# Stores of a planned kernel ordered two microseconds later, and a crossbar turn planned to land later

## The chip, the cores and the metric

One core of a Trainium2 chip runs the whole program. The metric is the device time of one execution in microseconds (us); lower is better. The engines that matter here are TensorE (PE for its matmuls, PEld for its weight loads), VectorE (DVE), ScalarE (ACT) and SyncE (SP), whose queue issues every DMA of this kernel. GpSimd (POOL) does small things.

## The reference

Eight sequences of 576 tokens go through attention in chunks of 64, a feed-forward net with a residual, and a gated convolution:

```python
scores = scale * np.matmul(q_c, k_c.transpose(0, 1, 2, 4, 3))
attn = softmax(scores); out = np.matmul(attn, v_c)          # 8 heads of 64, chunks of 64
...
xn = (x - mu) / np.sqrt(var + 1e-06) * g_ln
x = x + np.maximum(xn @ w_ch1, 0.0) @ w_ch2                 # 512 -> 2048 -> 512
...
gate_pre += conv_w[k][None, None, :] * xp[:, k:k + S, :]    # 5 taps along the tokens
gate = 1.0 / (1.0 + np.exp(-gate_pre))
return (gate * (x @ w_val)) @ w_out
```

## The kernel before

The 4608 tokens are cut into 9 blocks of 512 (b = 0 to 8) and 36 attention units of 128 tokens. Numbers are split into a high and a low part, so that a product is three matmuls. Blocks 0 and 1 go through the feed-forward net plainly. From block 2 on its first layer is done by Strassen's scheme: for each group g of 512 hidden columns seven products, named 2, 1, 6, 5, 3, 7, 4 (`hidden`, line 1303), each 12 matmuls of 256 columns. Their combined weights lie in HBM (`a_dram`) and are loaded, 512 KB for each product, into a ring of six rooms (names `late_a`, `load` at line 1325, DMA at L1327). Results go from PSUM through ACT (`shot`, L1347), DVE (`join`, L1354), and ACT and DVE again (`high` L1382, `low` L1385) into the second layer (L1412 to L1414).

When a block's output X is complete, `conv` (line 1616) does two things with it beside the next blocks. It computes the five taps of the gate: one ACT step (L1638) and four DVE steps (L1645) for each of four column groups f, in two rooms `u0` and `u1` by turns, and stores the result to HBM (`gd`, L1658). And `seven` (line 1424) makes the seven operands of the last stage: DVE differences (L1454), ACT high parts (L1472), DVE low parts (L1477), and a store of each (`x7d`, L1482) out of three rooms. A room is free again when its store has landed. Block 0's part is done later, from a copy in HBM (`x2d`): `seven_again` reloads it at L1525 and `conv_again` at L1577. The last stage (`val`, `proj`) reloads operands and gates.

From unit 8 on the attention probabilities are turned by a crossbar DMA: ACT takes the halves of the words apart (L682), SP issues the DMA transpose (L690), ACT puts them together (`pT`, L699).

No order is written by hand. Each step is an `Op` with an engine, a duration, dependencies and a priority, and `Plan.run` (line 55) plays them through as a list scheduler: an engine that is free takes the ready step of least priority value. The order of these picks is the order in which the instructions are emitted, and on the chip each engine keeps it: a step that waits holds up everything behind it on its engine, and SP's queue is one such order. An op becomes ready at the planned end of its dependency plus a hop: 80 ns behind DVE or ACT, 220 ns behind PE, 3500 ns behind an SP op (its landing), plus `more` of the op that ended. `slack` of the waiting op is added where the dependency is an SP op. These numbers alone decide the order; none of them is waited for on the chip, where semaphores do that.

Of the kernel before, what the change touches and what calls it, by code (L numbers as in the profile page):

```python
# [20 lines left out]


class Op:
    __slots__ = ("eng", "dur", "fn", "deps", "pri", "left", "after", "ready", "seq", "xfer", "more", "slack")

    def __init__(self, eng, dur, fn, deps, pri, seq):
        self.eng, self.dur, self.fn, self.pri, self.seq = eng, dur, fn, pri, seq
        self.deps = [d for d in dict.fromkeys(deps) if d is not None]
        self.after, self.ready, self.xfer, self.more, self.slack = [], 0.0, None, 0.0, 0.0


class Plan:
# [23 lines left out]
    def run(self):  # L56
        for op in self.ops:
            op.left = len(op.deps)
            for d in op.deps:
                d.after.append(op)  # L60
        free = {e: 740.0 if e == "SP" else 0.0 for op in self.ops for e in op.eng}
        ready = {e: [] for e in free}
        events = []
        done = set()

        def offer(op):
            for e in op.eng:
                heapq.heappush(ready[e], (op.pri, op.seq, op))

        for op in self.ops:  # L70
            if not op.left:
                offer(op)
        t, n, moved, landed = 0.0, 0, 0.0, []
        while n < len(self.ops):
            for e in free:
                if free[e] > t:
                    continue
                q = ready[e]
                while q and q[0][2].seq in done:
                    heapq.heappop(q)  # L80
                if not q:
                    spent = self.idle(t) if self.idle and e == "PE" else None
                    if spent:
                        free[e] = t + spent
                        heapq.heappush(events, (free[e], -1, None))
                    continue
                op = heapq.heappop(q)[2]
                done.add(op.seq)
                dur = op.dur[op.eng.index(e)] if isinstance(op.dur, tuple) else op.dur
                end = t  # L90
                for x, parts in op.xfer or ():
                    flying = landed[-self.LANES :]
                    if len(flying) == self.LANES:
                        end = max(end, flying[0][0])
                    for l, _ in flying:
                        if sum(m for z, m in flying if z > end) + parts > self.RING:
                            end = max(end, l)
                    turn = self.TURN if parts == P and landed and landed[-1][1] != P else 0.0
                    end += dur
                    moved = max(end + self.LAG, moved + turn) + x  # L100
                    landed.append((moved, parts))
                if not op.xfer:
                    end = t + dur
                free[e] = end
                if len(op.eng) > 1:
                    op.fn(e)
                else:
                    op.fn()
                n += 1
                for a in op.after:  # L110
                    if op.xfer:
                        wait = moved - end
                    else:
                        wait = 0.0 if a.eng == (e,) else max(self.HOP[e], self.HOP["PE"] if "PE" in a.eng else 0.0) + op.more
                        if e == "SP":
                            wait += a.slack
                    a.ready = max(a.ready, end + wait)
                    a.left -= 1
                    if not a.left:
                        heapq.heappush(events, (a.ready, a.seq, a))  # L120
                heapq.heappush(events, (free[e], -1, None))
            if n == len(self.ops):
                break
            t = max(t, events[0][0])
            while events and events[0][0] <= t:
                op = heapq.heappop(events)[2]
                if op is not None:
                    offer(op)
# [3 lines left out]
def chunk_attention_ffn_gated_conv(  # L132
# [385 lines left out]
    def unit(u):  # L518
# [3 lines left out]
        b, o = divmod(u, TB)  # L522
# [412 lines left out]
        def turned_probabilities():  # L935
            sp = op("ACT", 1250, apart, ex, bu)
            cp = op("SP", 600, crossbar, sp, su, p=pri - 20000.0)
            cp.more = 1000.0
            return op("ACT", 1370, together, cp)

        ep = turned_probabilities() if ready else None
# [490 lines left out]
    def seven(b, quad, reads, pri):  # L1432
# [29 lines left out]
        def split(i, m, src, *deps):  # L1462
# [21 lines left out]
            oh = add("ACT", 680, high, list(deps) + take(rt), pri)  # L1484
            ol = add("DVE", 690, low, [oh], pri)
            x7_store[b, m] = add("SP", 1300, store, [ol], pri)
            x7_store[b, m].more = 2000.0
            hold(rt, x7_store[b, m])
            if src:
# [81 lines left out]
    def conv_again(f):  # L1571
# [35 lines left out]
            oa = add("DVE", 760, more(i), [oa], pri)  # L1607
        hold(rt, oa)
        conv_store[0, f] = add("SP", 728, keep, [oa], pri)
        hold(at, conv_store[0, f])  # L1610

    def conv(b):
# [19 lines left out]
        for f in range(KD if b else 0):  # L1632
# [31 lines left out]
                oa = add("DVE", 760, more(i), [oa], pri)  # L1664
            last.append(oa)
            conv_store[b, f] = add("SP", 728, keep, [oa], pri)
            hold(at, conv_store[b, f])
        if b == 0:
            x2_store[b] = add("SP", 2900, store, done, pri)
# [441 lines left out]
```

## Time and profile before

| what | us |
|---|---|
| median of 3 runs | 1070.41 |
| lowest and highest | 1068.20, 1075.63 |
| profiled execution | 1070.03 |
| its span, first to last instruction | 1068.2 |

The rows below come from the profiled execution. Of its 1070.03 us the span is 1068.2; 1.83 us lie around it. The granted TensorE clock is 1.00 of full speed over the span, so no step of time is due to the clock. "Idle before" in a row is the time in which that engine did nothing before the instruction, with the instruction or DMA that ended it. A PE matmul's own duration contains its way through the array, so two that follow each other overlap: 12 matmuls of a product start over about 1.4 us.

### The profile page before, as it was taken

The page shows a single profiled execution, that of the slowest core. Times are in us where ns is not written, and L with a number is a line of the kernel's source. Part 1 is how long each engine was busy: PE and PEld are TensorE (multiplying, and loading weights), DVE is VectorE, ACT ScalarE, POOL GpSimd, SP SyncE. Part 2 cuts the span into 40 slices and gives each one's busy share as a digit, 9 for nine tenths or more (in the row PEclk, how much of TensorE's full clock was granted, in tenths as well). Part 3 has the DMA queues.
Part 4 walks back from the last instruction along what each step waited for, and adds up shares of the span by engine and source line. Part 5 has one row for each costly group of instructions (what it writes and reads, how often), then busy time and mean ns, then how long its engine had stood idle before and what let it go on. Part 6 is the DMA issues. An engine that isn't in the chain of part 4 may idle for free.

```text
span 1068.2 us, 22725 instructions
## 1 busy us (share of the span) xinstructions
PE 1053.9 (99%) x8950; PEld 951.4 (89%) x8950; DVE 856.4 (80%) x1464; ACT 540.3 (51%) x871; POOL 40.4 (4%) x77
## 2 busy tenths in 40 slices
PE   9999999999999999999999999999999999999998
PEld 8988888888899988889888898899898989999998
DVE  5888978888885888767878877878756889998785
ACT  5796634435354445445445543544443555655553
POOL 1011000000000000000000000000000000000000
PEclk9999999999999999999999999999999999999999
DMA  8995358667999899989989989998976988999852
GB/s 193 289 368 175 108 159 252 220 179 207 246 329 270 233 297 337 282 242 344 278 260 329 299 233 233 352 282 250 319 234 203 381 330 305 309 334 377 316 206 80
DMA packets 205905, 284.14 MB, mean 266 GB/s; under 512 B 99278, under 2 KB 151014, under 8 KB 205798
## 3 DMA queue, kind: packets, MB, share of 16 engines
q1 hardware_dynamic: 205798, 282.68, 84.6%
q8 instruction: 71, 1.16, 0.5%
q14 instruction: 36, 0.29, 0.1%
HBM read 207.64 MB, written 67.63 MB: 258 GB/s over the span
## 4 chain that ended last, share of the span: by engine, by line
PE 88%; DMA 4%; issue 2%; DVE 2%; ACT 2%; SPq 1%; POOL 0%; DVEq 0%; ACTq 0%; POOLq 0%
PE m L1255 24%; PE o L1255 8%; PE v L1255 8%; PE y L1034 7%; PE yA L1412 5%; PE yA L1414 5%; PE yB L1412 5%; PE yB L1414 4%; PE yA L1413 4%; PE yB L1413 4%; PE att L631 3%; PE att L604 3%; PE h L1010 3%; PE h L1012 2%; PE h L1011 2%
## 5 line engine op out<-in xcount | busy, mean ns | idle before, releaser
L1255 PEld LDWEIGHTS m<-late,late_a 128*128 128x128 f32 x2352 | 296.3, 188 | 22.5 <-DVE c_hl L1354 6.1
L1255 PE MATMUL m<-late,late_a 128*128 128x256 f32 x2352 | 303.3, 280 | 7.1 <-DMA late_a<-a 3.1
L1645 DVE SCALAR_TENSOR_TENSOR u_room<-X,cw_sb,u_room 128x516 f32<-128x516 f32 (+1 forms) x128 | 95.1, 747 | 10.4 <-ACT u_room L1638 7.9
L1034 PE MATMUL y<-hh,w 128*128 128x512 f32 x224 | 70.9, 398 | 0.0
L1354 DVE TENSOR_TENSOR c_hh<-c_hh,m 128x512 f32<-128x512 f32 x56 | 38.4, 685 | 36.6 <-PE m L1255 22.9
L1347 ACT ACTIVATE c_hh<-m 128x512 f32<-128x512 f32 x56 | 33.4, 596 | 54.9 <-PE m L1255 54.7
L1412 PE MATMUL yA<-late_h,w 128*128 128x512 f32 x148 | 59.4, 401 | 0.0
L1412 PE MATMUL yB<-late_h,w 128*128 128x512 f32 x148 | 59.0, 399 | 0.0
L1414 PE MATMUL yB<-late_h,w 128*128 128x512 f32 x148 | 58.1, 393 | 0.0
L1414 PE MATMUL yA<-late_h,w 128*128 128x512 f32 x148 | 58.0, 392 | 0.0
L1413 PE MATMUL yA<-late_h,w 128*128 128x512 f32 x148 | 58.0, 392 | 0.0
L1413 PE MATMUL yB<-late_h,w 128*128 128x512 f32 x148 | 57.8, 390 | 0.0
L1034 PEld LDWEIGHTS y<-hh,w 128*128 128x128 f32 x224 | 40.8, 188 | 8.4
L1287 ACT ACTIVATE late<-xs 128x512 fp32r<-128x512 f32 x49 | 30.4, 628 | 35.1 <-PE m L1255 20.6
L1010 PE MATMUL h<-xnt,w 128*128 128x512 f32 x112 | 45.4, 405 | 0.0
L770 POOL TENSOR_TENSOR rstd<-ve,neg_half 128x1 f32<-128x1 f32 x36 | 24.7, 687 | 541.8 <-DVE ve L750 541.4
L1012 PE MATMUL h<-xnt,w 128*128 128x512 f32 x112 | 44.2, 395 | 0.0
L1011 PE MATMUL h<-xnt,w 128*128 128x512 f32 x112 | 44.2, 394 | 0.0
L1034 PE MATMUL y<-hl,w 128*128 128x512 f32 x112 | 44.0, 393 | 0.0
L1382 ACT ACTIVATE late_h<-c_hh 128x512 fp32r<-128x512 f32 x38 | 23.9, 630 | 38.9 <-DVE c_hh L1354 38.2
L678 ACT ACTIVATE p<-p 128x512 f32<-128x512 f32 x33 | 20.8, 630 | 41.6 <-DVE p L670 23.6
L699 ACT ACTIVATE pT<-px 128x1024 uint16<-128x1024 uint16 x28 | 38.5, 1374 | 6.3 <-DMA px<-ps 6.1
(272 smaller groups left out, 2440.0 us busy)
## 6 DMA issues: line engine op xcount, KB each, us to landing
late_a<-a SPq DMA_DIRECT2D x196, 512.0 KB, 5.6
x7d<-late_x SPq DMA_DIRECT2D x42, 512.0 KB, 5.9
late_a<-x7d SPq DMA_DIRECT2D x39, 512.0 KB, 5.4
raw<-in_moe_w_ch_dram SPq DMA_DIRECT2D x32, 512.0 KB, 7.6
late<-x7d SPq DMA_DIRECT2D x24, 512.0 KB, 5.5
qk_room<-in_q_dram SPq DMA_DIRECT2D x100, 112.0 KB, 5.2
qk_room<-in_k_dram SPq DMA_DIRECT2D x100, 112.0 KB, 4.1
x7d<-x SPq DMA_DIRECT2D x21, 512.0 KB, 5.6
```

Source lines behind the costliest of these rows:

```text
L699: nc.scalar.activation(out=t.bitcast(U16).rearrange("p (x s) -> p s x", s=2), in_=st["turned"], func=AF.Copy)
L1010: nc.tensor.matmul(ps, wh, xh, start=(kk == 0), stop=False)
L1011: nc.tensor.matmul(ps, wh, xl, start=False, stop=False)
L1012: nc.tensor.matmul(ps, wl, xh, start=False, stop=(kk == KD - 1))
L1034: nc.tensor.matmul(ps, w[:, s], x, start=opens and n == 0, stop=closes and n == 2, skip_group_check=not b)
L1255: nc.tensor.matmul(ps[:, f], l, right(r, k), start=new and f == k == i == 0, stop=k == 1 and i == 2, skip_group_check=True,)
L1347: nc.scalar.activation(out=st[tag], in_=st[into], func=AF.Copy)
L1354: nc.vector.tensor_tensor(out=st[tag], in0=st[tag], in1=y, op=op)
L1412: nc.tensor.matmul(ps, wh, hh, start=opens and f == 0, stop=False)
L1413: nc.tensor.matmul(ps, wl, hh, start=False, stop=False)
L1414: nc.tensor.matmul(ps, wh, hl, start=False, stop=closes and f == 3)
L1645: nc.vector.scalar_tensor_tensor(out=a, in0=X[b][:, f, i : i + L], scalar=cw_sb[:, i, f : f + 1], in1=a, op0=ALU.mult, op1=ALU.add,)
```

## The change

An `Op` gets a field `behind`, zero by default. Where an op waits for a step that was not on SP, its planned ready time is put off by `behind`. It is set to 2000 ns for three kinds of store: the operands (`x7d`, L1482), the gates of block 0 (L1600) and the gates of the other blocks (L1658). The second edit raises `more` of the crossbar DMA from 1000 to 2500 ns, so the step that puts the turned words together is planned to be ready 6.0 us behind the DMA's issue step, where it was 4.5.

```diff
+                        else:
+                            wait += a.behind
...
-            cp.more = 1000.0
+            cp.more = 2500.0
...
             x7_store[b, m] = add("SP", 1300, store, [ol], pri)
+            x7_store[b, m].behind = 2000.0
             x7_store[b, m].more = 2000.0
...
         conv_store[0, f] = add("SP", 728, keep, [oa], pri)
+        conv_store[0, f].behind = 2000.0
...
             conv_store[b, f] = add("SP", 728, keep, [oa], pri)
+            conv_store[b, f].behind = 2000.0
```

Every engine issues the same instructions as before, in the same number; POOL's order is unchanged, and PE, DVE, ACT and SP have rows in other places from about unit 9 on. Nothing is moved ahead of that. Line numbers grow by 2 to 5.

The first place is PE at the turn from block 1's plain net to block 2's products. `h1_15` is the last hidden column tile of block 1, `m1_2_0` and `m2_2_0` are products 1 and 2 of block 2, group 0. Before:

```order
L1255 MATMUL m1_2_0_2957<-late0_1912,late_a2_0_2_2135 128x256 x12
L1010 MATMUL h1_15_2907<-xnt1_0_1206,w27_1619 128x512
L1011 MATMUL h1_15_2907<-xnt1_0_1206,w27_1619 128x512
L1012 MATMUL h1_15_2907<-xnt1_0_1206,w27_1619 128x512
L1255 MATMUL m2_2_0_2989<-late0_1912,late_a2_0_2_2135 128x256 x12
```

After, on PE at the same place:

```order
L1012 MATMUL h1_15_2899<-xnt1_0_1206,w27_1619 128x512
L1013 MATMUL h1_15_2899<-xnt1_0_1206,w27_1619 128x512
L1014 MATMUL h1_15_2899<-xnt1_0_1206,w27_1619 128x512
L1257 MATMUL m1_2_0_2963<-late0_1912,late_a2_0_2_2148 128x256 x12
L1257 MATMUL m2_2_0_2979<-late0_1912,late_a2_0_2_2148 128x256 x12
```

Product 1 now stands between the last matmuls of `h1_15` and product 2; before it stood ahead of both.

The second place is SP in block 6, group 2, while block 5's gates and operands are stored. `a3_1` is the weight of product 1 of group 3, `gd5` and `x7d5` are the stores of block 5. Before:

```order
L1482 DMA x7d5_2_120<-late_x7_1_1_3132 128x1024
L1327 DMA late_a2_0_2_2135<-a3_2_207 128x1024
L1658 DMA gd5_80<-u_room_185 128x320
L1658 DMA gd5_80<-u_room_185 128x192
L1327 DMA late_a2_0_6_2162<-a3_1_208 128x1024
L1482 DMA x7d5_6_122<-x7_5_6_7962 128x1024
L1327 DMA late_a2_0_6_2162<-a3_6_209 128x1024
L1482 DMA x7d5_3_124<-late_x7_1_1_3132 128x1024
```

After, on SP at the same place:

```order
L1484 DMA x7d5_2_120<-late_x7_1_1_3134 128x1024
L1329 DMA late_a2_0_2_2148<-a3_2_207 128x1024
L1329 DMA late_a2_0_6_2175<-a3_1_208 128x1024
L1329 DMA late_a2_0_6_2175<-a3_6_209 128x1024
L565 DMA qk_room_148<-in_q_dram 32x4x224 x4
L1662 DMA gd5_80<-u_room_185 128x320
L1662 DMA gd5_80<-u_room_185 128x192
L1484 DMA x7d5_6_122<-x7_5_6_7987 128x1024
L1484 DMA x7d5_3_124<-late_x7_1_1_3134 128x1024
```

Two weight loads and four reads of q now go ahead of the gate store that they stood behind.

The third place is block 5, group 1, from product 7 to product 4 on PE, and what DVE does there. `att27` is an attention unit's small products, `m1_5_1` with `late1` is product 7, with `late2` product 4, and `m1_5_2` is product 1 of the next group. PE before:

```order
L1255 MATMUL m1_5_1_6410<-late1_2982,late_a2_0_2_2135 128x256 x12
L631 MATMUL att27_6672<-v26_6500,pT26_6609 64x64 x16
L631 MATMUL att27_6672<-kT27_6607,qT27_6564 64x64 x16
L1255 MATMUL m1_5_2_6707<-late0_1912,late_a2_0_6_2162 128x256 x12
L1255 MATMUL m1_5_1_6410<-late2_3004,late_a2_0_2_2135 128x256 x12
```

PE after:

```order
L1257 MATMUL m1_5_1_6390<-late1_2959,late_a2_0_2_2148 128x256 x12
L633 MATMUL att27_6672<-v26_6503,pT26_6637 64x64 x16
L633 MATMUL att27_6672<-kT27_6605,qT27_6579 64x64 x16
L1414 MATMUL yA_5_6429<-late_h2_1_0_3289,w12_1072 128x512
L1415 MATMUL yA_5_6429<-late_h2_1_0_3289,w12_1072 128x512
L1416 MATMUL yA_5_6429<-late_h2_1_0_3289,w12_1072 128x512
L1257 MATMUL m1_5_1_6390<-late2_3043,late_a2_0_2_2148 128x256 x12
```

Three matmuls of the second layer take the place of the next group's product 1 between 7 and 4. On DVE the sum that product 4 waits for is `c5_1_hl0`, and product 1 of the next group waits for `c5_1_hh1`. DVE before:

```order
L1477 TENSOR_TENSOR late_x7_1_1_3132<-X4_4717,late_x7_1_1_3132 128x512
L1645 SCALAR_TENSOR_TENSOR u_room_185<-X4_4717,cw_sb_74,u_room_185 128x516 x2
L1354 TENSOR_TENSOR c5_1_hh1_6587<-c5_1_hh1_6587,m5_5_1_6594 128x512
L1645 SCALAR_TENSOR_TENSOR u_room_185<-X4_4717,cw_sb_74,u_room_185 128x516 x2
L1354 TENSOR_TENSOR c5_1_hl0_6623<-c5_1_hl0_6623,m1_5_1_6410 128x512
```

DVE after:

```order
L1356 TENSOR_TENSOR c5_1_hh1_6586<-c5_1_hh1_6586,m5_5_1_6592 128x512
L1479 TENSOR_TENSOR x7_4_5_6645<-t4_6623,x7_4_5_6645 128x512
L1649 SCALAR_TENSOR_TENSOR u_room_185<-X4_4717,cw_sb_74,u_room_185 128x516
L1387 SCALAR_TENSOR_TENSOR late_h2_1_0_3289<-c5_1_hh1_6586,late_h2_1_0_3289 128x2x256
L1356 TENSOR_TENSOR c5_1_hl0_6617<-c5_1_hl0_6617,m1_5_1_6390 128x512
```

Four tap steps stood ahead of `c5_1_hl0` and two ahead of `c5_1_hh1`; now one stands ahead of the first and none ahead of the second. Block 6, group 1 has the same move on PE; on DVE there the two taps ahead of `c6_1_hl0` become one tap and one low part (L1385).

## Rows read from the trace of the kernel before

**Rows 1.** The page's first part: busy time, share of the span and instructions of each engine.

```profile
PE 1053.9 (99%) x8950; PEld 951.4 (89%) x8950; DVE 856.4 (80%) x1464; ACT 540.3 (51%) x871; POOL 40.4 (4%) x77
```

**Rows 2.** Windows: us; PE, PEld, DVE, ACT, POOL busy (instructions); clock; DMA share; GB/s.

```profile
100.00:250.00 150.00, 148.59 (x1140) 120.93 (x1139) 124.38 (x225) 69.42 (x106) 8.00 (x17) 1.00 0.59 176
250.00:850.00 600.00, 594.22 (x5080) 534.11 (x5078) 474.37 (x825) 284.63 (x459) 21.76 (x36) 1.00 0.93 281
850.00:1064.00 214.00, 213.77 (x1738) 208.53 (x1736) 176.35 (x282) 115.22 (x204) 0.00 (x0) 1.00 0.80 287
```

**Rows 3.** Waits of PE: who waited for whom, us in total, times, longest.

```profile
PE m L1255 <- DMA late_a<-a: 3.1, 2, 1.6
PE m L1255 <- DVE c_hl L1354: 2.1, 3, 1.0
```

**Rows 4.** Timeline at the turn to block 2: start, us, what [idle before, releaser].

```profile
244.13 1.58 PE L1255 MATMUL m<-late,late_a 128*128 128x256 f32 x12
...
245.54 0.39 PE L1010 MATMUL h<-xnt,w 128*128 128x512 f32 x1
...
246.01 0.39 PE L1012 MATMUL h<-xnt,w 128*128 128x512 f32 x1
...
247.07 0.69 DVE L1022 SCALAR_TENSOR_TENSOR hl<-h,hh 128x512 fp32r<-128x512 f32 x1 [3.22 <-ACT hh L1018]
...
247.81 0.86 PE L1255 MATMUL m<-late,late_a 128*128 128x256 f32 x5 [1.41 <-DVE hl L1022]
```

**Rows 5.** Timeline of SP, block 6, group 2, and of PE there.

```profile
667.95 0.59 SPq L1327 DMA_DIRECT2D late_a<-a  x1
670.99 0.86 SPq L1658 DMA_DIRECT2D gd<-u_room  x2
671.95 0.44 SPq L1327 DMA_DIRECT2D late_a<-a  x1
...
678.15 2.12 PE L1255 MATMUL m<-late,late_a 128*128 128x256 f32 x16 [1.46 <-DMA late_a<-a]
```

**Rows 6.** The window around rows 5, columns as in rows 2.

```profile
665.00:680.00 15.00, 13.54 (x91) 12.27 (x91) 11.16 (x19) 7.32 (x13) 1.49 (x2) 1.00 1.07 362
```

**Rows 7.** Timeline of block 5, group 1.

```profile
558.48 0.73 ACT L1638 ACTIVATE u_room<-X,cw_sb 128x516 f32<-128x516 f32 x1 [2.39 <-DMA gd<-u_room]
...
559.25 1.55 DVE L1645 SCALAR_TENSOR_TENSOR u_room<-X,cw_sb,u_room 128x516 f32<-128x516 f32 x2 [2.42 <-ACT u_room L1638]
...
561.45 1.68 PE L1255 MATMUL m<-late,late_a 128*128 128x256 f32 x12 [0.49 <-DVE c_hh L1354]
...
563.51 1.68 PE L1255 MATMUL m<-late,late_a 128*128 128x256 f32 x12 [0.38 <-DVE c_hl L1354]
```

**Rows 8.** Timeline of block 6, group 1.

```profile
653.31 0.72 ACT L1638 ACTIVATE u_room<-X,cw_sb 128x516 f32<-128x516 f32 x1 [4.88 <-DMA gd<-u_room]
...
655.53 0.68 DVE L1354 TENSOR_TENSOR c_hl<-c_hl,m 128x512 f32<-128x512 f32 x1
...
656.27 1.65 PE L1255 MATMUL m<-late,late_a 128*128 128x256 f32 x12 [0.78 <-DVE c_hl L1354]
```

**Rows 9.** Timeline of SP, block 3, group 2, and of PE there.

```profile
389.31 0.38 SPq L1525 DMA_DIRECT2D u_room<-x2d  x1
...
390.77 0.42 SPq L1327 DMA_DIRECT2D late_a<-a  x1
...
396.87 0.36 PE L1255 MATMUL m<-late,late_a 128*128 128x256 f32 x1 [1.61 <-DMA late_a<-a]
```

**Rows 10.** Waits of ACT: as rows 3.

```profile
ACT u_room L1638 <- DMA gd<-u_room: 25.8, 10, 5.8
...
ACT pT L699 <- DMA px<-ps: 6.1, 5, 2.4
```

**Rows 11.** Timeline of SP and PE, block 4, group 0.

```profile
425.13 1.00 SPq L1525 DMA_DIRECT2D u_room<-x2d  x1
...
429.49 1.55 PE L1255 MATMUL m<-late,late_a 128*128 128x256 f32 x12
```

More of the change, by code (lines that the diff above doesn't have):

```diff
@@ L23 @@
 class Op:
-    __slots__ = ("eng", "dur", "fn", "deps", "pri", "left", "after", "ready", "seq", "xfer", "more", "slack")
+    __slots__ = ("eng", "dur", "fn", "deps", "pri", "left", "after", "ready", "seq", "xfer", "more", "slack", "behind")
     def __init__(self, eng, dur, fn, deps, pri, seq):
@@ L28, in __init__ @@
         self.deps = [d for d in dict.fromkeys(deps) if d is not None]
-        self.after, self.ready, self.xfer, self.more, self.slack = [], 0.0, None, 0.0, 0.0
+        self.after, self.ready, self.xfer, self.more, self.slack, self.behind = [], 0.0, None, 0.0, 0.0, 0.0
 class Plan:
```

## The prediction

> **What bounds the kernel now.** I read the page's busy line first. TensorE's matmuls are busy for 1053.9 us, 99% of the span of 1068.2, no other engine for more than 80% beside its weight loads [rows 1]. So the reader should see at once how little a new order can win: PE's instructions are the same in number and kind, and only its idle time, 1068.2 - 1053.9 = 14.3 us, is to be had. The windows say where that lies. The order changes from about unit 9 on, so the stretch from 100 us to the last matmul counts: there PE is idle for 1.41 + 5.78 + 0.23 = 7.42 us [rows 2]. The other 6.9 us lie in the first 100 us, where no instruction moves, and behind the last matmul. A measurement of this kernel can tell about 1% from no change, which is 10.7 us; even with every idle microsecond in reach gone, the change stays inside that on the fast side.
>
> The waits of PE come next. The largest are two waits for a product's weights (3.1 us in two), then sums that DVE makes for a product (2.1 us in three) [rows 3]; then comes one wait for a low part at the turn to block 2 (1.41) [rows 4]. I looked each of them up in the timeline, because a store planned later can help a wait only where that store, or the order that follows from it, stands in that wait's chain.
>
> **The change part by part.** It removes and adds nothing; each part is a move.
>
> The turn to block 2. Product 2 needs the bank out of which DVE's low part of h1_15 reads. The last matmul of h1_15 starts at 246.01, the low part ends at 247.07 + 0.69 = 247.76, and product 2 starts at 247.81 after 1.41 us of idleness [rows 4]. In the new order product 1 stands between. Its 12 matmuls took from 244.13 to 245.54, 1.41 us [rows 4], and fill just the time that was idle. Term: -1.4; bounds -1.41, the whole wait, and 0, should the low part be later by as much because product 1's own operand or weight is not there.
>
> The weight load in block 6. The load that releases product 1 of group 3 was issued at 671.95, behind a gate store that SP held from 667.95 + 0.59 on and issued at 670.99, when DVE had ended its last tap; PE started the product at 678.15, 6.2 us behind the issue, after 1.46 us of idleness [rows 5]. Now the load stands straight behind the one of 667.95, ahead of that store. The six-room ring allows it: the room's last reader is product 6 of group 2, which PE has left by then. So it goes out at about 668.6, 3.3 us sooner, and a landing 3.3 us sooner covers 1.46. Term: -1.46; bounds -1.46 and 0. The zero is real: in this window the DMA engines show a share of 1.07 and 362 GB/s [rows 6], so a load that starts sooner may wait in the engines instead of in SP's queue. Against that stands that the bytes of the gate store and of an operand's store are now behind it, and I take the full term, being twice covered. The Trainium skill (DMA: Bandwidth & Descriptors, Where 436 GB/s comes from) puts the limit between HBM and SBUF at about 358 GB/s for one core, which this window's 362 has reached; by that rule alone the order of issues in such a window gains nothing and the term would be 0.
>
> What the four q reads and the two gate store pieces now wait for is off PE's path: q is turned more than a group later, and the gates are read back in the last stage.
>
> Block 5, group 1. ACT's tap step waited 2.39 us for a gate store's landing, and DVE's taps behind it; PE then stood 0.49 us for c_hh and 0.38 us for c_hl [rows 7]. In the new order c_hh is ahead of the taps, so its 0.49 goes. Product 4 comes sooner in PE's order: PE is free of the attention unit at 561.45 - 0.49 = 560.96, and three second-layer matmuls of 512 columns, which start 0.23 us apart (245.54 to 246.01 for two [rows 4]), put it at 561.65. The gate store that ACT waits for now stands behind one more load, some 0.5 us of issue; ACT's step would then end at 558.9 + 0.7 = 559.6, one tap of 1.55 / 2 = 0.77 at 560.4, a low part and the sum (0.68 each, as the sum in rows 8) at 561.7. So about 0.1 us of idleness is left of 0.87. Term: -0.75; bounds -0.87 and +0.5.
>
> Block 6, group 1. Here the move costs. ACT's wait for the gate store is 4.88 us, DVE's sum c_hl, behind the taps, runs at 655.53 and PE waits 0.78 us for it [rows 8]. That store keeps its place in SP's queue, so the landing stays. A low part takes the second tap's place ahead of c_hl, 0.1 us less. But three matmuls (0.69 us) stand between products 7 and 4 where a product of 1.4 us stood, so PE arrives 0.7 us sooner at the same wait. Term: +0.6; bounds 0 and +0.7.
>
> Block 3, group 2. PE waits 1.61 us for a weight issued at 390.77, just behind a reload of x2d at 389.31 which itself waits until the gate store of the room that it fills has landed [rows 9]. In the new order one weight load goes ahead of that gate store, so the reload, and the weight behind it, come later by that one issue (up to 1.5 us if it takes as long as from 389.31 to 390.77 here); but the next gate store, which stood between reload and weight, now follows the weight, which gives back about 0.9. I take 0; bounds -0.9 and +1.1.
>
> The crossbar. The planned landing decides only where ACT's last step of a unit stands among its other work. ACT waits for it 6.1 us in five of 28 units, at most 2.4 [rows 10], and in none of PE's large waits is that step the releaser [rows 3]. Cost nothing; its cover is ACT's idle half (51% busy [rows 1]), and without that a share of 6.1 us is the most it could give and 1.5 us for a unit the most that it could take.
>
> The tap steps of the other blocks wait longer only if their room's store goes out later in fact; the plan knows of it and moves them. I cost this at nothing; the rivals price it.
>
> Sum: -1.4 - 1.46 - 0.75 + 0.6 + 0 = -3.0 us. From the profiled execution, 1070.03 - 3.0 = 1067.0; the median of the runs shown lies 0.4 above that execution, so 1067.4 is the forecast.
>
> **The rivals.** First, a swap of stalls: the gains come, but a list scheduler's new order opens as many small waits as it shuts. For it speaks that what PE waits for before is a handful of places out of the 7 x 4 x 7 = 196 products of blocks 2 to 8, each an accident of order; against it that the waits for weights were only two, so most loads have room to be moved. It ends at no change: 1070.4, give or take 1.5.
>
> Second, slower: reloads of x2d and stores in front of weights. In block 4, group 0, the loads of products 1, 6, 5, 3 and 7 now stand behind two stores and a reload of x2d that before went out behind them, the reload at 425.13. If these keep their old times, product 1's weight goes out at 425.13 + 1.00 = 426.1 and frees PE 6.2 us later (as in rows 5), at 432.3, while PE started that product at 429.49 [rows 11]: +2.8. The same pattern in block 3 costs its +1.1, and block 6 its +0.6; with none of the gains but the turn to block 2 (-1.4), that is +3.1 and 1073.5. It decides once SP holds such a reload for over some 3 us longer than the plan thinks. For it speaks that SP stood still for the reload of rows 9; against it that the new order has those stores' DVE work earlier too.
>
> Third, the gate rooms. ACT's tap steps wait 25.8 us in ten places for gate stores [rows 10], and in two of them PE paid: 0.87 in block 5 and 0.78 in block 6 [rows 7, 8]. If the ten waits all grow by the two microseconds that the stores were put off and half of that shows on PE, +10 us: 1080. The plan moves those steps too, so this is unlikely.
>
> Fourth, more gain than the idle time holds. The Trainium skill (Perfetto Trace Analysis, Identifying the Most-Contended Engine) holds that matmul busy time says little of what is left, and that the weight loads' busy share is the better measure. Weight loads are busy 89% [rows 1], 534 of 600 us in the middle [rows 2], which would leave 66 us there where the matmul rows leave 5.8. If a sixth of that were to be had, the time would be 1059. The rows of the middle speak against it: the loads' share is low where the 512-column matmuls, not the loads, set the pace, and there are no gaps between those.
>
> That the change does nothing at all is out: PE's order itself moves at the places shown.
>
> **How the numbers follow.** Forecast, between -5 and -1 us of the profiled time: 0.50. Swap of stalls: 0.27. Reloads and stores in front of weights: 0.16. Gate rooms: 0.04. More than the idle time: 0.03. The likeliest alone would give 1065 to 1069.5. For 8 in 10 I go down to 1063.0, where all 7.42 us are gone (1070.41 - 7.4), and up to 1075.0, past the second rival. Faster by over 1% holds only the last rival, 0.03; slower by over 1% (beyond 1081) the tail of the third, and some of the second at more places than I found, 0.04; within 1% the rest, 0.93.
>
> **What would show it.** Right: PE's list of waits no longer has the 1.4 us for hl, product 1 of block 6, group 3 starts without a wait, and PE's idle time from 100 us on is near 4.5 us instead of 7.4. The block 6, group 1 wait should have grown to about 1.4. Wrong: a new wait of PE for late_a, most likely in block 4, group 0 or in block 3, or ACT's wait for gate stores well above 25.8 us with PE waiting for c_hl in more than three places. PE idle time above 9 us would mean that the order lost more than it won.

## The result and the profile after

The changed kernel took 1074.93 us in the median (20 runs, 1071.51 to 1078.93), the kernel before 1069.57 beside it (20 runs). The ratio is 1.0056 with a 95% interval of 1.0044 to 1.0068: slower by 0.56%; the medians lie 5.4 us apart, where a gain of 3.0 us was forecast. That is inside 1%, but on the other side. (The ratios here and below are the recorded ones, which are not quotients of the medians.)

The profiled execution took 1076.13 us, its span is 1074.2. The busy line of the page of the changed kernel:

```profile
PE 1059.8 (99%) x8950; PEld 957.5 (89%) x8950; DVE 856.9 (80%) x1464; ACT 540.4 (50%) x871; POOL 40.0 (4%) x77
```

The same 8950 matmuls now keep PE busy 5.9 us longer than in [rows 1]. Part of the time it ran slower. The windows show where, in the columns of [rows 2]:

```profile
100.00:250.00 150.00, 149.99 (x1141) 121.94 (x1140) 124.04 (x224) 66.78 (x102) 9.52 (x19) 1.00 0.59 170
250.00:850.00 600.00, 592.10 (x5048) 532.43 (x5047) 469.64 (x822) 280.45 (x457) 21.46 (x36) 0.99 0.94 279
850.00:1070.00 220.00, 219.44 (x1777) 213.98 (x1776) 184.07 (x288) 122.85 (x210) 0.00 (x0) 1.00 0.80 288
399.86:403.27 3.41, 3.41 (x18) 3.41 (x18) 0.40 (x1) 1.11 (x2) 0.00 (x0) 0.50 0.77 279
591.00:594.40 3.40, 3.40 (x17) 3.40 (x18) 0.59 (x1) 0.66 (x2) 0.00 (x0) 0.50 0.98 348
```

The first three answer to [rows 2]. PE's idle time from 100 us on is 0.01 + 7.90 + 0.56 = 8.47 us, where it was 7.42. The last two are two stretches in which the granted clock was 0.50 of full speed (1.2 in place of 2.4 GHz); the kernel before has none ahead of its last microseconds. Each takes 3.41 us for work of half that, so each costs 1.7 us. Measured on the products: the 24 matmuls behind either wait take 4.59 us (from 399.27 and from 590.90), and 2.98 in the kernel before (from 396.87).

PE's waits, answering to [rows 3], and ACT's for the gates' rooms, answering to the first of [rows 10]:

```profile
PE m L1257 <- DMA late_a<-a: 7.1, 4, 2.8
...
PE m L1257 <- DVE c_hl L1356: 1.0, 1, 1.0
...
ACT u_room L1642 <- DMA gd<-u_room: 15.6, 8, 3.4
```

The waits for sums that DVE makes went from 2.1 us to 1.0, ACT's waits for gate stores from 25.8 to 15.6, and the wait for `hl` is gone. But PE's wait for weights went from 3.1 us in two places to 7.1 in four. Three of them are for product 1 of a group. SP and PE in block 3, answering to [rows 9]:

```profile
385.54 0.32 SPq L1329 DMA_DIRECT2D late_a<-a  x1
385.95 2.14 SPq L1662 DMA_DIRECT2D gd<-u_room  x2
392.46 0.38 SPq L1528 DMA_DIRECT2D u_room<-x2d  x1
392.93 1.14 SPq L1329 DMA_DIRECT2D late_a<-a  x1
...
399.27 3.48 PE L1257 MATMUL m<-late,late_a 128*128 128x256 f32 x17 [2.75 <-DMA late_a<-a]
```

SP has issued the gate store at 385.95 + 2.14 = 388.09 and then issues nothing for 4.4 us. The next DMA in its queue is the reload of x2d into the room out of which that store reads, and it may not start until the store has landed. The weight load of 392.93 stands behind it. In the kernel before a weight load stood between store and reload, and SP stood still for a microsecond less:

```profile
383.28 1.10 SPq L1658 DMA_DIRECT2D gd<-u_room  x2
384.47 1.48 SPq L1327 DMA_DIRECT2D late_a<-a  x1
```

There the reload went out at 389.31 [rows 9], 3.4 us behind 384.47 + 1.48. The half clock of 399.86 comes right behind PE's 2.75 us without work. The second and third wait are in block 5, ahead of groups 1 and 3:

```profile
531.55 2.70 SPq L692 DMA_TRANSPOSE px<-ps  x1
534.30 2.00 SPq L565 DMA_DIRECT2D qk_room<-in_k_dram  x4
536.40 1.58 SPq L1329 DMA_DIRECT2D late_a<-a  x3
...
542.39 2.86 PE L1257 MATMUL m<-late,late_a 128*128 128x256 f32 x23 [1.72 <-DMA late_a<-a]
...
577.93 1.74 SPq L1662 DMA_DIRECT2D gd<-u_room  x2
579.71 0.91 SPq L1484 DMA_DIRECT2D x7d<-late_x  x1
580.72 1.33 SPq L1329 DMA_DIRECT2D late_a<-a  x2
...
590.90 4.36 PE L1257 MATMUL m<-late,late_a 128*128 128x256 f32 x22 [2.30 <-DMA late_a<-a]
```

In both places PE had no wait before. Product 1's load is the second of the three of 536.40, and of the two of 580.72; a crossbar turn, four reads of k, a gate store and an operand's store stand ahead of it. The fourth wait (block 8) is 0.3 us.

So the two profiles differ like this, from 100 us on: 1.0 us more idle time and 2 x 1.7 us of half clock, 4.4 us in all. Matched instruction by instruction, PE is 6.1 us later at the end, of which 2.35 come in the first 100 us, where both kernels issue the same instructions in the same order; the other 3.75 stand against these 4.4. The start is no part of the change: the same 12 matmuls of `warm_h` take 1.50 us in the kernel before (from 9.45) and 2.49 in the changed one (from 12.09), and 2.62 in the experiment b_pool63, which begins like the kernel before. So this pair of profiles shows some two thirds of the 5.4 us between the medians. Place by place, by how much PE is later in the changed kernel at matmuls that stand at the same place in both orders:

| place, up to (us in the kernel before) | PE later by, us | step | term forecast |
|---|---|---|---|
| first 100 us | 2.35 | +2.35 | none |
| turn to block 2, 311 | 1.24 | -1.1 | -1.4 |
| block 3, 421 | 4.21 | +3.0 | 0 |
| block 4, 515 | 3.90 | -0.3 | none |
| block 5, ahead of group 1, 553 | 6.03 | +2.1 | none |
| block 5, group 1, 583 | 4.57 | -1.5 | -0.75 |
| block 5, ahead of group 3, 631 | 8.72 | +4.2 | none |
| block 6, group 1, 670 | 7.78 | -0.9 | +0.6 |
| block 6, group 3, 692 | 6.06 | -1.7 | -1.46 |
| last matmul | 6.10 | 0 | none |

The gains came, 5.2 us of them. The losses, 9.3 us, stand at three loads for which the sum had 0 or no term.

### The profile page after: what moved, and what is told of

Read it like the earlier page. It is cut to its first block, busy times and chain, and to the rows that moved or that the text cites. A ratio compares the mean times of both kernels' runs of the same rounds, so it can differ in the third digit from the quotient of the medians.

```text
span 1074.2 us, 22706 instructions
## 1 busy us (share of the span) xinstructions
PE 1059.8 (99%) x8950; PEld 957.5 (89%) x8950; DVE 856.9 (80%) x1464; ACT 540.4 (50%) x871; POOL 40.0 (4%) x77
## 4 chain that ended last, share of the span: by engine, by line
PE 95%; DMA 3%; SPq 1%; DVE 1%; issue 0%; ACT 0%; POOL 0%; DVEq 0%; ACTq 0%; POOLq 0%
PE m L1257 24%; PE o L1257 8%; PE v L1257 8%; PE y L1036 7%; PE yA L1414 5%; PE yA L1416 5%; PE yA L1415 5%; PE yB L1414 4%; PE yB L1416 4%; PE yB L1415 4%; PE att L606 4%; PE att L633 4%; DMA late_a<-a 3%; PE h L1012 3%; PE h L1014 2%; PE h L1013 2%
## 5 line engine op out<-in xcount | busy, mean ns | idle before, releaser
L1257 PEld LDWEIGHTS m<-late,late_a 128*128 128x128 f32 x2352 | 299.9, 190 | 23.9 <-DVE c_hl L1356 4.0
L1257 PE MATMUL m<-late,late_a 128*128 128x256 f32 x2352 | 306.5, 281 | 8.1 <-DMA late_a<-a 7.1
L1293 DVE TENSOR_TENSOR late<-xs,late 128x512 fp32r<-128x512 f32 x49 | 33.0, 686 | 7.9 <-ACT late L1289 7.8
```

What stands on the lines that cost most here:

```text
L1257: nc.tensor.matmul(ps[:, f], l, right(r, k), start=new and f == k == i == 0, stop=k == 1 and i == 2, skip_group_check=True,)
```

## The experiments

Theory A: a few loads of weights come late because SP's queue, which issues in order, stands still or is busy ahead of them; a long wait of PE then also costs half clock. Rivals: the loss is spread (B), it is the crossbar's later landing (C), or the DMA engines are at capacity there, and whatever is put off makes a wait of the same size (F).

| kernel | runs | median us | ratio to before, 95% interval |
|---|---|---|---|
| changed kernel | 20 | 1074.93 | 1.0056 (1.0044 to 1.0068) |
| p_behind | 7 | 1077.53 | 1.0054 (1.0031 to 1.0077) |
| p_gates | 12 | 1074.88 | 1.0042 (1.0022 to 1.0062) |
| p_x7 | 12 | 1070.91 | 0.9998 (0.9980 to 1.0016) |
| p_more | 12 | 1071.20 | 1.0006 (0.9988 to 1.0025) |
| p_nogates | 12 | 1070.84 | 1.0024 (1.0007 to 1.0041) |
| s_33 | 8 | 1072.69 | 1.0035 (1.0017 to 1.0053) |
| s_53 | 12 | 1073.13 | 1.0030 (1.0012 to 1.0047) |
| s_all | 12 | 1069.86 | 1.0008 (0.9989 to 1.0027) |
| s_five | 12 | 1070.62 | 1.0019 (0.9998 to 1.0041) |
| g_two | 12 | 1073.96 | 1.0035 (1.0012 to 1.0058) |
| r_pool | 12 | 1070.06 | 1.0007 (0.9980 to 1.0033) |
| b_keep | 12 | 1070.66 | 1.0011 (0.9985 to 1.0037) |
| b_ahead | 12 | 1069.42 | 0.9999 (0.9982 to 1.0016) |
| b_pool | 12 | 1067.39 | 0.9976 (0.9954 to 0.9997) |
| bg_pool | 12 | 1068.79 | 0.9993 (0.9968 to 1.0019) |
| bm_pool | 12 | 1066.09 | 0.9967 (0.9950 to 0.9985) |
| b_pool63 | 12 | 1066.69 | 0.9962 (0.9942 to 0.9981) |

The expectations count each wait for weights some 0.16 us longer than the rows do (2.92, 1.89 and 2.46 for 2.75, 1.72 and 2.30).

**Which edit.** Five kernels have parts of the change. p_behind has the two `behind` edits, p_gates and p_x7 one each, p_more the crossbar alone; p_nogates leaves the gates' out.

Of these four lines p_more drops the last three, p_behind the first, p_gates the first two, p_x7 the first and the last two, p_nogates the last two:

```diff
+            cp.more = 2500.0
+            x7_store[b, m].behind = 2000.0
+        conv_store[0, f].behind = 2000.0
+            conv_store[b, f].behind = 2000.0
```

> Only the two `behind` edits (x7 stores and gate stores); the crossbar's `more` is back at 1000. Theory A (the loss is a few longer waits of PE for the first weight load of a group, because SP has other transfers ahead of it, and a clock at half for about 1.7 us behind the longest of them): at block 3 group 2 to 3 the x2d reload stands ahead of a3_1 as in the changed kernel, so its wait is near 2.9 us with the half clock behind it (+1.15 +1.6); at block 5 group 1 the reads of k stand behind px25 as in the changed kernel, so its 1.9 us are there; the 1.4 us wait for hl at the turn to block 2 is back; block 6 group 3's 1.6 us are gone. Sum 1069.6 + 2.75 + 1.9 - 1.6 = 1072.6 us, up to 1075 if block 5 group 3 waits too. Rival B (the loss is spread over the whole program by the other order on ACT and DVE): no wait above 2 us, the time between 1071 and 1075 all the same. Rival C (the crossbar's later landing does it all): 1069.6 us, within 1 us.

> Only the crossbar's `more` of 2500; no store is ordered by `behind`. Theory A: the turn to block 2 gains 1.1 to 1.4 us, block 3 group 3's wait stays near 1.8 us with no fall of the clock (the order there is that of before, with one more 512 KB load ahead of a3_1: up to 0.5 more), block 5 group 1 waits up to 1.9 us (the crossbar and the reads of k ahead of a1_1), block 5 group 3 waits up to 2.5 us with 1.7 of half clock (px27 ahead of the gate's stores, as in the changed kernel). Sum from 1069.6 - 1.3 = 1068.3 to 1069.6 - 1.3 + 1.9 + 4.2 = 1074.4 us; middle 1071.5. Rival B: between 1069 and 1071 with no long wait. Rival C: 1074 to 1075 us, the whole loss.

> `behind` on the stores of operands (x7) alone. Theory A: block 3 group 3 keeps the order of before (wait 1.8, no half clock), block 5 group 1 has the crossbar and the reads of k ahead of a1_1 (+1.9), block 6 group 3's 1.6 us are gone, the 1.4 us at the turn to block 2 stay: 1069.6 + 1.9 - 1.6 = 1069.9 us, 1068 to 1072. Rival B: half of the loss, 1072 us. Rival C: 1069.6 us, and no wait moves.

> `behind` on the stores of gates alone. Theory A: block 3 group 3 has the order of the changed kernel (gates' stores and the x2d reload ahead of a3_1): wait near 2.9 us and the clock at half behind it, +2.75; block 5 group 1 has the order of before but for px25 ahead of one gate store (0 to +0.5); block 6 group 3's 1.6 us are gone: 1069.6 + 2.75 - 1.6 = 1070.8 us, 1069.5 to 1073. Rival B: half of the loss, 1072 us, without long waits. Rival C: 1069.6 us, and no half clock.

> The changed kernel without `behind` on the gates' stores: the x7 stores' `behind` and the crossbar's `more` of 2500 stay. Theory A (the gates' part is the loss, since it puts the gate store next to the x2d reload that waits for it, and p_gates alone cost 0.42%): 1069.7 + 0 to -1.5 = 1068 to 1071 us, no wait over 2 us at block 3 group 3 and no half clock. Rival E (the three edits only lose together, one with the other): 1073 to 1075 us.

The gates' `behind` carries most of the loss: 0.42% alone, 0.54% with the x7 stores'. The other two alone cost nothing that these runs can tell, so C falls. The sizes of A were too low for p_behind (1077.5 against at most 1075) and p_gates (1074.9 against at most 1073), and p_gates' profile does not lose where A said: its wait in block 3 is 1.71 us without half clock, and a wait of 3.14 us for DVE in block 5, with half clock behind it, is new. p_nogates' median lies in A's range (1070.84), but its ratio of 0.24% leaves out 1: the harmless two together lose something, and its profile has a 2.7 us wait with half clock in block 3 although the order there is the old one. One profile's wait at one place is no constant of the order: here it is 1.7 to 3.5 us in five profiles with store and reload side by side (changed kernel, p_behind, p_gates, s_53, b_keep), and 2.7, 1.7, 1.6, 1.2 and at most 0.6 in five with a load between them (p_nogates, g_two, kernel before, p_x7, p_more).

**Which place.** These leave all engines' orders as they are and move single DMAs in SP's queue; the plan's times are not touched, only what SP emits is held back until another op has gone. s_33, s_53 and s_all on the changed kernel:

```diff
 block 3 (s_33, s_all)
-u_room<-x2d
 late_a<-a3_1
+u_room<-x2d
 block 5 group 3 (s_53, s_all)
+late_a<-a3_1
 gd4, x7d4_2, late_a<-a3_2
-late_a<-a3_1
 block 5 group 1 (s_all)
+late_a<-a1_1
 px25, qk_room<-in_k x4, late_a<-a1_2
-late_a<-a1_1
```

> The changed kernel with one DMA of SP moved: in block 3 the load of a3_1 (the weights of product 1 of group 3) stands ahead of the x2d reload, which waits 4.30 us for the gate's store to land in the room that it overwrites. All other engines keep their order. Theory A (PE waits 2.92 us there because the load stands behind that wait in SP's queue): a3_1 is issued near 388.1 us of its span in place of 392.93, PE's wait there goes to 0 to 0.5 us, and the half clock behind it (about 1.7 us) goes too where it came: 1074.9 - 2.9 - 1.7 = 1070.3 us, 1070 to 1073. Rival B (the loss is spread over the program): PE's wait goes, the time stays at 1074 to 1076 because other waits take it up.

> The changed kernel with one DMA of SP moved: in block 5 the load of a3_1 stands ahead of a pair of x7 and a3_2 transfers (x7d4_2's store and the load of a3_2), not behind them. Theory A: a3_1's issue comes 1 to 3 us earlier and it lands in 7 to 8 us in place of 9.5, so PE's wait of 2.46 us there goes, and the half clock behind it: 1074.9 - 2.5 - 1.7 = 1070.7 us, 1070.5 to 1073. Rival B: 1074 to 1076, the wait moves to another place. Rival D (the load is late because the room it writes comes free late, not because of the queue): SP waits at it, the issue stays within 1 us of where it was, and the wait stays above 1.5 us.

> The changed kernel with three DMAs of SP moved: the load of product 1's weights goes ahead in block 3 group 3 (past the x2d reload), in block 5 group 1 (past the turned probabilities px25, the reads of k and a1_2) and in block 5 group 3 (past x7d4_2 and a3_2). Theory A: the three waits of 2.92, 1.89 and 2.46 us go, and the two stretches of half clock with them (2 x 1.7): 1074.9 - 7.3 - 3.4 = 1064.2 us, 1063 to 1068, faster than both kernels; no granted clock below 1.0 before the end. Rival B: above 1072, since a planned program with other waits takes up what is gained.

In the three profiles each wait is gone where its load was moved ahead. Where it was not, block 3's stays (2.8 us in s_53), and those of block 5 are now larger, now smaller (2.5 and 1.1 us in s_33). s_33 came out in A's range (1072.69), s_53 just above it (1073.13). s_all wins back 0.48 of the 0.56%. But it is 5.7 us above A's sum: 7.3 us of waits went, others came. PE's waits in s_all:

```profile
PE att L632 <- DVE xn L817: 2.9, 2, 1.8
PE att L659 <- DMA v<-in_v_dram: 2.0, 1, 2.0
...
PE m L1283 <- DMA late_a<-a: 1.1, 1, 1.1
```

Single swaps thus take a wait away and let another in, as rival B had it, though B's times (above 1072 for s_all, 1074 to 1076 for the other two) did not come. s_five moves two more loads ahead (a3_1 in block 6; a3_4 and v20 ahead of two x7 stores and the reads of k):

> The changed kernel with the three loads of s_all ahead, and two more: in block 6 a3_1 ahead of x7d5_2's store and a3_2 (PE waits 1.3 us for it in s_all), and at the end of block 3 a3_4 and v20 ahead of two x7 stores and the reads of k of unit 21 (PE waits 2.0 us for v20 in s_all, with the half clock behind it). Theory A: 1069.9 - 1.3 - 2.0 - up to 1.7 = 1065 to 1067 us, faster than before. Rival F: 1069 to 1071 us, other waits take their place.

It missed A too and came out at F's figure (1070.62): in its profile 2.5 us of waiting for a turned k came at the same spot, where the reads of k had been put back. The next two work on the kernel before: b_keep makes its SP order in block 3 like that of the changed kernel, b_ahead moves the two loads of rows 3 ahead.

```diff
 b_keep
+late_a<-a3_2
 gd2 (piece 2)
-late_a<-a3_2
 u_room<-x2d
 b_ahead, block 3 (and block 6 past a gd5 pair)
+late_a<-a3_1
 u_room<-x2d, gd2 (piece 3)
-late_a<-a3_1
```

> The kernel before with one DMA of SP moved: in block 3 the load of a3_2 goes ahead of the pair of stores of gate piece 2 (gd2), so that these stand right in front of the x2d reload that waits for them, as in the changed kernel. Theory A (a gate store ordered later, next to the reload that overwrites its room, is what makes the load of a3_1 late): the reload's wait grows from 3.28 to over 4 us, a3_1 is issued 1 to 1.5 us later against PE, PE's wait for it grows from 1.77 to near 3 us, and a stretch of half clock follows in a part of the runs: 1069.6 + 1.2 + 0 to 1.7 = 1070.8 to 1072.5 us. Rival G (SP's place of that store does not matter, the reload waits for something else): wait and time as before, 1069.6 within 0.7.

> The kernel before with the load of a3_1 moved ahead at two places: in block 3 past the x2d reload and a pair of gate stores, in block 6 past a pair of gate stores. Theory A: PE's two waits for late_a of before (1.77 and 1.62 us) go and nothing else changes: 1069.6 - 3.4 = 1066.2 us, 1065.5 to 1068. Rival F (the DMA engines are at capacity there, and the transfer that is put back makes another wait of the same size): 1069 to 1070.5 us, with a new wait for v, x or another weight within 30 us behind.

b_keep moves one DMA and shows the whole chain. SP, PE and the window behind it:

```profile
384.43 0.32 SPq L1350 DMA_DIRECT2D late_a<-a  x1
384.85 1.81 SPq L1681 DMA_DIRECT2D gd<-u_room  x2
391.73 0.38 SPq L1548 DMA_DIRECT2D u_room<-x2d  x1
392.20 1.66 SPq L1681 DMA_DIRECT2D gd<-u_room  x2
393.95 0.78 SPq L1350 DMA_DIRECT2D late_a<-a  x1
...
398.93 3.81 PE L1278 MATMUL m<-late,late_a 128*128 128x256 f32 x22 [3.52 <-DMA late_a<-a]
...
400.42:403.83 3.41, 3.41 (x42) 3.19 (x44) 0.69 (x1) 1.74 (x4) 0.00 (x0) 0.50 1.03 420
```

SP stands still for 391.73 - 386.66 = 5.1 us, the weight load comes 3.2 us later than in [rows 9], PE waits 3.52 us in place of 1.61, and the half clock follows. All 12 of its runs have a mean granted clock below 1.000. Its median is 1.7 us above that of the kernel before in the same job (1068.96), where A had 1.2 to 2.9, but the interval of the ratio holds 1: the chain is shown, its price only as a median. b_ahead misses A and comes out at F's figure (1069.42). In its profile the first of its two waits is gone and the second down to 0.3 us, but a wait of 4.1 us comes at the end of block 3, with 6.8 us of half clock at its end:

```profile
PE att L656 <- ACT late L1312: 4.1, 1, 4.1
...
421.36:428.19 6.83, 6.01 (x78) 5.81 (x79) 3.56 (x6) 2.40 (x6) 0.00 (x0) 0.50 1.00 345
```

The row names an ACT step, but the first read of v20, issued at 416.06, lands at 422.05, and PE goes on at 422.18. This execution took 1074.12 us, the longest of its 12, so it shows one way in which the gain is lost and not its usual size.

That left two causes open: the DMA engines at capacity (share 1.00), or SP's queue, which in b_ahead still stands still for the reload, so that what is behind it, v20 among them, goes out late.

**The queue or the engines.** g_two takes `behind` from block 2's gate stores alone. In the other three POOL issues the four reloads of x2d in place of SP (in bg_pool also the gate stores of blocks 1 to 8); the bytes and the other engines' orders are the same, though these DMAs then also go through another DMA queue (1.05 MB in q0 of r_pool's page, which the kernel before does not have).

```diff
 g_two
-            conv_store[b, f].behind = 2000.0
+            conv_store[b, f].behind = 0.0 if b == 2 else 2000.0
 r_pool (on the changed kernel), b_pool (on the kernel before)
-                nc.sync.dma_start(out=st[q], in_=x2_dram[...])
+                nc.gpsimd.dma_start(out=st[q], in_=x2_dram[...])
```

> The changed kernel without `behind` on the gate stores of block 2 alone: only a handful of SP's rows in block 3 change, back to the order of before (gate store, a3_2, reload, gate store, a3_1). Theory A: the wait at block 3 group 3 goes from 2.92 to about 1.8 us and the half clock behind it is rarer: 1074.9 - 1.1 - 0 to 1.7 = 1072 to 1073.8 us. Rival H (the gates' loss lies at the other blocks' gate stores): 1074.5 to 1075.5 us.

> The changed kernel with the four x2d reloads of block 3 and 4 issued by POOL in place of SP; nothing else moves. Theory A (SP's queue stands still for 4.30 us behind the reload's wait): a3_1 is issued near 388 us, PE's wait of 2.92 us there goes, the reload itself is not later than before, so no wait takes its place: 1074.9 - 2.9 - up to 1.7 = 1070.3 to 1072 us. Rival F (DMA engines at capacity: what is issued earlier lands no earlier): PE's wait at block 3 group 3 stays over 1.5 us or a new one over 2 us comes by 425 us, and the time stays above 1073.

> The kernel before with the four x2d reloads issued by POOL. Theory A: PE's wait of 1.77 us at block 3 group 3 goes and none comes: 1069.3 - 1.8 = 1067.5 us, 1066.5 to 1068.5. Rival F: 1069 to 1070 us.

> The kernel before with the x2d reloads and all gate stores of blocks 1 to 8 issued by POOL, so that neither stands in SP's queue. Theory A: both waits of rows 3 (1.77 and 1.62 us) go: 1069.3 - 3.4 = 1065.9 us, 1065 to 1067.5, faster than both kernels. Rival F: 1069 to 1070 us, or slower where POOL's own issue of a store takes longer than SP's and the reload behind it on POOL waits more.

r_pool has the changed kernel's order and none of its loss in block 3. SP, POOL and PE there:

```profile
383.10 0.32 SPq L1329 DMA_DIRECT2D late_a<-a  x1
383.51 1.44 SPq L1662 DMA_DIRECT2D gd<-u_room  x2
385.85 0.32 SPq L1329 DMA_DIRECT2D late_a<-a  x1
...
390.45 0.92 POOL L1528 DMA_DIRECT2D u_room<-x2d  x1 [13.15 <-DMA late_a<-a]
...
392.54 4.26 PE L1257 MATMUL m<-late,late_a 128*128 128x256 f32 x36
```

The reload still waits for the store, 390.45 against 384.95, but nobody stands behind it. The load of a3_1 goes out at 385.85, PE runs three products on end without a wait, and up to 460 us no wait above 0.3 us takes its place. Later this profile does lose again: behind 1.26 us of waiting for ACT at 561.03 the clock is at half for 3.41 us. The ratio falls from 1.0056 to 1.0007. The same edit on the kernel before gives 1067.39, forecast 1067.5, a gain of 0.24% whose interval leaves out 1, though in its profile PE's wait in block 6 is 2.60 us, with half clock behind it, where it was 1.46. So F falls for block 3: the bytes in that stretch are the same. Whether the reload's other DMA queue has a part in it was not tried apart. With the gate stores on POOL too (bg_pool) A's sum of 1065.9 is missed and F's range too; PE then waits for ACT's copies of sums and for a normalised tile that come late (2.4 and 2.2 us). g_two lies between A and H at 1073.96: its wait in block 3 is 1.74 us without half clock, as A had it, but it still waits in block 5, 2.2 us of it for DVE.

The last two look for a version faster than both kernels: b_pool with the crossbar's `more` of 2500, and b_pool with a3_1 of block 6 ahead of a3_2 and a gate store.

> The kernel before with the x2d reloads issued by POOL, and the crossbar's `more` at 2500 as in the change (no `behind`). Theory A: the turn to block 2 gains its 1.1 to 1.4 us on top of b_pool's 1067.4: 1066.0 us, 1065 to 1067.5, faster than both kernels. Rival: the other order that it brings in blocks 5 and 6 takes that back, 1067 to 1069 us.

> b_pool with the load of a3_1 of block 6 moved ahead of a3_2 and a pair of gate stores in SP's queue. Theory A: PE's wait there (2.76 us in b_pool's profile, 1.62 in the kernel before, with half clock behind it in b_pool) goes: 1067.4 - 1.6 to -2.8 = 1064.6 to 1066 us. Rival: it comes back as another wait in block 6, 1067 to 1068.5 us.

bm_pool: 1066.09, A's number. b_pool63 lies between its two forecasts at 1066.69; block 6's wait is gone in its profile, and one of 1.7 us for weights has come in block 5. Both are faster than both kernels, by 0.33 and 0.38% against the kernel before, with intervals that leave out 1. In bm_pool's profile the clock never falls ahead of the end, and its largest waits are for DVE and ACT, not for weights:

```profile
PE m L1255 <- DVE h L1385: 1.8, 1, 1.8
...
PE m L1255 <- ACT c_hh L1347: 1.4, 1, 1.4
```

## Why the prediction was wrong

**What bounds the kernel.** PE does, as said. The failed step is the one behind it: "I looked each of them up in the timeline", each of the waits that PE had before. The sum priced these and no place where PE had none. Of the loss three waits are for weights, and two of these three (1.72 and 2.30 us in block 5) stand where PE had started without a wait. A load with no wait had little slack either: in block 5, group 1, it was issued 5.5 us ahead of its product and landed 0.6 us before it (532.25, 537.18, 537.78); ahead of group 3 it landed 0.7 us before (583.13, 583.86). These two places cost 2.1 and 4.2 us in the table above, and the sum had no term for either.

**The turn to block 2, -1.4.** Right; the step in the table is -1.1. Product 1 fills the gap, and no wait is left:

```profile
246.90 0.40 PE L1014 MATMUL h<-xnt,w 128*128 128x512 f32 x1
247.14 3.27 PE L1257 MATMUL m<-late,late_a 128*128 128x256 f32 x24
```

It is the crossbar's edit that brings this order, which was costed at nothing: p_more has it alone, p_behind keeps the wait of 1.4. On b_pool it is worth the 1.3 us between the medians of b_pool and bm_pool, though these come from two jobs.

**Block 6, a3_1, -1.46.** Right in this profile: the load goes out with its neighbours and the product starts without a wait.

```profile
675.98 3.34 SPq L1329 DMA_DIRECT2D late_a<-a  x3
...
682.93 3.25 PE L1257 MATMUL m<-late,late_a 128*128 128x256 f32 x27
```

But here the load lands at 684.10 for a product, the second in this row, that starts at 684.32, and r_pool and s_33, with this same order in SP there, wait 1.29 and 2.01 us at this product. A gain of one landing is not a gain of the order.

**Block 5, group 1, -0.75, and block 6, group 1, +0.6.** The first came: neither of [rows 7]'s waits is left. The second had the wrong sign, its wait of [rows 8] is gone as well: ACT's tap step there, which had waited 4.88 us for a gate store, starts at 658.32 without a wait, while the term kept that landing where it was. ACT's waits for gate stores shrank as a whole (25.8 to 15.6).

**Block 3, 0 with bounds -0.9 and +1.1.** Mis-sized: PE's wait grew by 1.14 us, the upper bound, and the half clock of 1.7 us came on top, which no term held. The text had the mechanism in its two halves, that the reload waits for the store's landing and that the load behind it comes later, and then let the next gate store's 0.9 us cancel it.

**The rivals.** The second was the nearest: SP holding a reload in front of weights. Its place was wrong (block 4, group 0 has no wait), its +1.1 for block 3 right, and its price for the whole, +3.1, is 2.3 us short of the 5.4. It got 0.16. The first had the other half, that new waits open where old ones shut, and let the two cancel; what was said against it, that "most loads have room to be moved", was the error in short. The gate rooms fell, and so did a gain beyond the idle time.

**The range.** The median of 1074.93 lies just under the 1075.0 that the range for 8 in 10 ends at. That is luck of the base: the kernel before ran at 1069.57 beside it and at 1070.41 in the runs shown, and as a difference the range reached to +4.6 where +5.4 came.

**The clock.** The granted clock of 1.00 in the profile before was taken as given. Over 148 runs of the kernel before that stood beside these experiments, 66 had a mean granted clock of 1.000 (median 1068.5 us) and 57 one of 0.998 or below (median 1071.7). Of the 20 runs of the changed kernel two are at 1.000 (1071.5 and 1074.2) and 15 at 0.998 or below (median 1076.1). So a part of the loss is clock, and a part is there without it. An estimate from the recorded clocks: their means, 0.9990 over the 148 and 0.9971 over the 20, stand for 1.1 and 3.1 us lost to half clock, so some 2 us of the loss are clock and the other 3 are not.

**The DMA engines' limit.** 358 GB/s, from the Trainium skill (DMA: Bandwidth & Descriptors, Where 436 GB/s comes from), was weighed against the block 6 term. The Trainium skill (HBM Reference, Specifications (TRN2)) gives that figure for two cores that share a domain and about 425 for a core alone; the 420 GB/s in b_keep's window agrees with the second. The prediction's 358 was the wrong limit for one core alone.

Open stays what each of block 5's two waits is worth in the median, why p_gates loses without the wait in block 3, and why p_nogates loses 0.24%.

## What to carry to other kernels

A DMA that must wait for another's landing holds back everything behind it on the engine that issues it. In this plan an op on SP that follows an op on SP is ready at once: the 3500 ns for a landing are added only for a follower on another engine. So the plan put store and reload side by side and did not see the 4 to 5 us for which the queue stood still. Give such a DMA a queue on which nothing urgent stands; to plan its landing is the other way, which was not tried. Moving one load ahead of it gave back 0.21% (s_33) or nothing (b_ahead).

When an order changes, price the places that have no wait too: for each load in front of the bounding engine, how long ahead of its use it is issued, against how long it takes to land. And look at the granted clock of several runs: here a wait of PE could be paid twice.

## What was not expected of the hardware

The half clock came at or just behind a wait of PE: of 2.75 and 2.30 us in the changed kernel, 3.52 in b_keep, 4.1 in b_ahead; but not behind 1.72 us in the changed kernel, 1.61 before, nor behind one of 2.5 in s_33. The length of the wait does not decide it in these runs: in r_pool, p_x7 and p_behind it came some 2 us behind waits of 1.26, 1.34 and 1.36 us, and not behind one of 2.61 in p_behind. With 1.7 us for a stretch it can cost as much as the wait.

POOL's queue took the reloads without a loss, while DVE is busy 80% of the span: in r_pool they land 4.2 to 7.9 us behind their issue, and in the kernel before, from SP, the two whose landing is recorded 6.9 and 7.7. The Trainium skill (DMA: Bandwidth & Descriptors, Issuing engines are not separate DMA queues) says that issuing from several engines only saves the time of the issue. As to bandwidth the runs give no sign against it; but r_pool and b_pool show more than issue time, 0.49 and 0.24% of the kernel, and r_pool's rows show why in block 3: a DMA that waits for its room no longer holds the others. The Trainium skill (SBUF — State Buffer, SBUF: two separate sides) warns of DMAs issued from GpSimd beside some VectorE operations; no run here shows such a stall for these four reloads.
